# A routed expert layer with one static width for each place in an order by token count, and a second MLP whose first block runs in two parts

## The chip, the cores and the metric

The kernel runs on one core of one Trainium2 chip. The metric is the time of one execution on the device in microseconds (us). Lower is better.

## The reference

Three layers follow one another on 1536 tokens of 512 features. Only the second and the third are touched here.

```python
# 1. retention attention with a decay per head -> x [1536, 512]   (not touched)
# 2. each token goes to the one expert of 8 with the largest logit
logits = x @ w_gate                                # [1536, 8]
expert_idx = np.argmax(logits, axis=1)
gate_w = softmax(logits)[arange(N), expert_idx]
for e in range(8):
    mask = expert_idx == e
    h = np.maximum(x[mask] @ w1[e], 0.0)           # 512 -> 1024
    out[mask] = gate_w[mask, None] * (h @ w2[e])   # 1024 -> 512
# 3. a dense MLP
h = x @ w_in                                       # 512 -> 2048
return ((h - np.tanh(h)) @ w_out)                  # 2048 -> 512
```

`w_in` and `w_out` of the third layer arrive as float64, all other inputs as float32. With the inputs that the reference draws by default the eight experts get 195, 205, 194, 205, 168, 157, 227 and 185 tokens.

## The kernel before, in words

Every large product is taken in three matmuls: each float32 operand is split into a high part of TensorE's reduced float32 type (a cast on ACT) and a low part (the rest, a subtraction on DVE, both in `split`, L141 to L147), and high by high, low by high and high by low are added up in PSUM. So a weight tile costs one DMA, one ACT cast and one DVE subtraction before TensorE can use it. The weight tile is the stationary operand in the expert layer and in the first product of the second MLP; each matmul loads its own 128x128 weights.

The program has three stages.

The attention and routing stage handles 128 tokens in each of 12 steps. It finds each token's expert and its place there, and GpSimd scatters the scaled rows into `xs_d`, a DRAM buffer with room for 1536 rows of each expert (`scatter`, L62). It also decodes the first five of 32 float64 tiles.

The expert stage runs over n = 0 to 63: expert n // 8, feature tile n % 8 of 1024 = 8 x 128 (from L797). Each expert reads WT = 240 rows of its region of `xs_d` (`x_load`), transposes them on TensorE (`x_trans`), and multiplies with 240 moving columns for every expert. At step n, `e_first(n)` makes 12 matmuls with w1 and a ReLU, and `e_second(n - 2)` makes 12 with w2. The experts run in the order 0 to 7. After an expert's eighth tile its 240 result columns are copied from PSUM to `ysort` at the column `starts` of that expert (L639 on ACT, L641 on DVE); the next expert overwrites the columns beyond its count. `finish_routing` (L481) turns the eight counts into `starts` and a flag `over`, which is set if a count lies above WT or below 128; a second pass over windows of 256 tokens then replaces the result. The weights come by the queue of SyncE in the order of `fetch` (L787), some five steps ahead. The rows of an expert and the weights share that queue, and everything on it is issued in order.

The 32 float64 tiles are decoded beside this: `decode_load` (512 KB each, two buffers), `decode_math` (two ACT passes for the sign, two DVE passes for the bits), `decode_end` (an ACT pass for the magnitude and a GpSimd multiplication). One tile is decoded in every second step. From n = 52 on, once the last tile is decoded, `m_split` splits one tile in each step.

The second MLP (from L956) has three windows of 512 tokens and 16 feature tiles of 128 each: 48 steps. Step n is 12 matmuls `m_first` (L865), an approximation of h - tanh(h) in six ACT and six DVE operations (`g_head`, `g_body`, `g_high`, `g_low`), and, two steps later, 12 matmuls `m_second` (L945) that add up in four PSUM banks `outp` over the 16 tiles. The remaining splits of weight tiles are put into the DVE chain of a step as fillings: the list `fill` is taken from in two gaps of the chain of the next step, and what is left runs at its end. `pre` counts the tiles split so far; step n brings it to 2n + 8. `y_split` splits the tokens of the next window, and the last step of a window copies its four banks to `ysort` and scatters them to the output. All engine queues run in the order in which the program is written.

## Time and profile before

| | before |
|---|---|
| median of 3 runs | 561.08 us (560.43 to 564.28) |
| the profiled execution's own time | 558.93 us |
| span of its trace | 557.2 us |
| busy PE, PE weight loads, DVE, ACT, GpSimd | 95%, 83%, 82%, 67%, 21% |
| mean granted TensorE clock | 0.987 |

The profiled execution is 1.73 us longer than its span, and 2.15 us shorter than the median. PE is TensorE's matmul row, PEld its row of weight loads, which run beside the matmuls. Times in the rows below are microseconds from the start of the span unless marked ns; "L133" is line 133 of the kernel, and "x" counts instructions. A row's "idle before" is the time in which its engine waited, and the arrow names what it waited for.

### The profile page before, as it was taken

How to read it: one execution, taken by the hardware profiler on the slowest of the kernel's cores; microseconds unless marked ns; L12 is line 12 of the kernel's file. 1: busy time of each engine (PE TensorE's matmuls, PEld its weight loads, DVE VectorE, ACT ScalarE, POOL GpSimd, SP SyncE). 2: the span in 40 equal slices, each digit the busy share in tenths (PEclk: the TensorE clock that was granted, in tenths of full speed). 3: DMA queues.
4: the chain of work that ended last, by engine and by line, in shares of the span. 5: the costliest groups of instructions: out<-in, count | busy, mean ns of one | idle time of the engine just before them, and what ended most of it. 6: DMA issues, size and time to landing. Idle time of an engine off the chain costs nothing.

```text
span 557.2 us, 10218 instructions
## 1 busy us (share of the span) xinstructions
PE 530.3 (95%) x3709; PEld 465.1 (83%) x3709; DVE 455.3 (82%) x866; ACT 374.3 (67%) x750; POOL 114.5 (21%) x139
## 2 busy tenths in 40 slices
PE   6999889999999999999989999999999999999991
PEld 5878768999999999999968888888888888888881
DVE  5988896899989899899679988987767697767670
ACT  2445655698788799898577878765555676565650
POOL 3656444054434322321000000003000003000002
PEclk8899999999999999999999999999999999999997
DMA  5999574999999999993000000002000002000002
GB/s 136 266 280 271 150 226 151 339 323 288 319 287 266 292 315 333 289 340 116 1 0 1 1 2 0 1 0 78 0 2 0 1 1 76 0 1 0 1 1 81
DMA packets 75660, 72.89 MB, mean 131 GB/s; under 512 B 30160, under 2 KB 60880, under 8 KB 75600
## 3 DMA queue, kind: packets, MB, share of 16 engines
q1 hardware_dynamic: 73248, 65.84, 41.1%
q0 software_dynamic: 2352, 6.31, 3.1%
q8 instruction: 31, 0.51, 0.4%
q14 instruction: 29, 0.24, 0.2%
HBM read 63.73 MB, written 8.39 MB: 129 GB/s over the span
## 4 chain that ended last, share of the span: by engine, by line
PE 56%; issue 16%; DMA 11%; DVE 8%; ACT 5%; POOL 2%; SPq 1%; POOLq 0%; DVEq 0%; ACTq 0%
PE mhp L865 17%; PE outp L945 16%; PE yp L633 10%; PE ehp L606 3%; PE ehp L607 3%; PE ehp L605 3%; DMA w1r<-in_moe_w_dram 3%; DMA w2r<-in_moe_w_dram 3%; DVE at L288 2%; DMA tok_d<-toks,cpi 2%; ACT qt L247 2%; DMA k<-in_k_dram 1%; POOL out_dram L64 1%; DMA raw<-in_moe_w_in_dram 1%; DVE state L312 1%
## 5 line engine op out<-in xcount | busy, mean ns | idle before, releaser
L633 PE MATMUL yp<-hb,w2h 128*128 128x240 f32 x512 | 89.9, 276 | 0.0
L874 ACT ACTIVATE u<-mhp 128x512 f32<-128x512 f32 x48 | 28.7, 597 | 80.4 <-PE mhp L865 80.3
L865 PE MATMUL mhp<-yh,mh 128*128 128x512 f32 x192 | 75.2, 392 | 1.9 <-ACT yh L145 1.9
L633 PEld LDWEIGHTS yp<-hb,w2h 128*128 128x128 f32 x512 | 76.9, 189 | 0.0
L865 PE MATMUL mhp<-yh,ml 128*128 128x512 f32 x192 | 74.7, 389 | 0.0
L606 PE MATMUL ehp<-xh,w1l 128*128 128x240 f32 x256 | 71.2, 278 | 1.1 <-DVE w1l L146 0.7
L633 PE MATMUL yp<-hb,w2l 128*128 128x240 f32 x256 | 70.7, 276 | 1.4 <-DVE w2l L146 1.3
L605 PE MATMUL ehp<-xh,w1h 128*128 128x240 f32 x256 | 70.7, 276 | 0.0
L607 PE MATMUL ehp<-xl,w1h 128*128 128x240 f32 x256 | 70.3, 275 | 0.0
L896 DVE SCALAR_TENSOR_TENSOR s<-s,u 128x512 f32<-128x512 f32 x48 | 33.1, 690 | 45.3 <-ACT s L876 45.3
L64 POOL DMA_INDIRECT out_dram<-ysort,idx x12 | 11.7, 974 | 282.8 <-ACT ysort L950 279.1
L138 POOL TENSOR_TENSOR dw<-da,sg 128x512 f32<-128x512 f32 x32 | 43.9, 1372 | 104.1 <-ACT da L137 82.9
L945 PE MATMUL outp<-mh,gl 128*128 128x512 f32 x192 | 54.0, 395 | 0.0
L945 PE MATMUL outp<-ml,gh 128*128 128x512 f32 x192 | 54.0, 395 | 0.0
L945 PE MATMUL outp<-mh,gh 128*128 128x512 f32 x192 | 53.7, 394 | 0.0
L146 DVE TENSOR_TENSOR w1l<-w1r,w1h 128x512 fp32r<-128x512 f32 x64 | 51.4, 803 | 1.8 <-ACT w1h L145 0.4
L146 DVE TENSOR_TENSOR w2l<-w2r,w2h 128x512 fp32r<-128x512 f32 x64 | 52.4, 819 | 0.3
L865 PE MATMUL mhp<-yl,mh 128*128 128x512 f32 x192 | 51.7, 391 | 0.0
L606 PEld LDWEIGHTS ehp<-xh,w1l 128*128 128x128 f32 x256 | 48.2, 188 | 2.6 <-DVE w1l L146 2.5
L633 PEld LDWEIGHTS yp<-hb,w2l 128*128 128x128 f32 x256 | 48.2, 188 | 1.9 <-DVE w2l L146 1.9
L605 PEld LDWEIGHTS ehp<-xh,w1h 128*128 128x128 f32 x256 | 48.2, 188 | 0.0
L607 PEld LDWEIGHTS ehp<-xl,w1h 128*128 128x128 f32 x256 | 48.2, 188 | 0.0
(144 smaller groups left out, 1214.1 us busy)
## 6 DMA issues: line engine op xcount, KB each, us to landing
w1r<-in_moe_w_dram SPq DMA_DIRECT2D x64, 256.0 KB, 6.8
w2r<-in_moe_w_dram SPq DMA_DIRECT2D x64, 256.0 KB, 6.7
raw<-in_moe_w_in_dram SPq DMA_DIRECT2D x16, 512.0 KB, 7.3
raw<-in_moe_w_out_dram SPq DMA_DIRECT2D x16, 512.0 KB, 6.4
q<-in_q_dram SPq DMA_DIRECT2D x12, 256.0 KB, 5.2
v<-in_v_dram SPq DMA_DIRECT2D x12, 256.0 KB, 5.5
k<-in_k_dram SPq DMA_DIRECT2D x11, 256.0 KB, 5.1
xr<-xs_d SPq DMA_DIRECT2D x8, 256.0 KB, 7.2
```

The lines of the kernel that those rows point to most:

```text
L64: ins = pool.indirect_dma_start(out=dst[:, :], out_offset=bass.IndirectOffsetOnAxis(ap=ix.bitcast(U32), axis=0), in_=src, in_offset=None)
L138: pool.tensor_tensor(out=w, in0=a.bitcast(F32), in1=sg, op=ALU.mult)
L146: dve.tensor_tensor(out=lo, in0=src, in1=hi.bitcast(F32), op=ALU.subtract)
L247: act.copy(out=o, in_=src)
L605: pe.matmul(hp, lhsT=ah, rhs=xh, start=(kk == 0), stop=False)
L606: pe.matmul(hp, lhsT=al, rhs=xh, start=False, stop=False)
L607: pe.matmul(hp, lhsT=ah, rhs=xl, start=False, stop=(kk == KD - 1))
L633: pe.matmul(o, lhsT=a, rhs=b, start=(f == 0 and i == 0 and m == 0), stop=(f == EF - 1 and m == 2), skip_group_check=True)
L865: pe.matmul(hp[:, j, :], lhsT=a[:, sl], rhs=b, start=(i == 0), stop=(i == 3 * KD - 1))
L874: act.activation(out=u, in_=hp, func=ACTF.Square)
L896: dve.scalar_tensor_tensor(out=s1, in0=s1, scalar=B1, in1=u, op0=ALU.add, op1=ALU.mult)
L945: pe.matmul(outp[w][i], lhsT=a[:, sl], rhs=b, start=(fs[j] == 0 and m == 0), stop=done)
```

## The change

The experts get an order: expert 0 first, then the others by falling token count. `finish_routing` computes the rank of each expert by comparing a key (eight times the count, plus a tie break) pairwise, the start column of each by adding the counts of those in front, and sorts counts, expert numbers and starts by rank into `byrank`. The place in the order, not the expert, now has a static width: 240, 240, 220, 212, 206, 200, 196, 192. SyncE reads the expert number of a place from `byrank_i` into a register (`expert`) and addresses weights and rows with it. `finish_routing` moves from step 2 to the end of step 0, the rows of the second expert are loaded at step 1 instead of step 0, and at step 0 `fetch` stays within expert 0. Both halves of an expert's result are copied to `ysort` by ACT.

Of the 32 float64 tiles 24 are decoded in the expert stage. The eight others are loaded in the second MLP in halves of 256 KB, decoded at steps 2, 5, 8, 11, 13, 15, 17 and 19 with the bit operations as fillings (`late_work`), and split two steps later. The first window of the second MLP runs feature tiles 0 to 11, then the second window runs 0 to 15, then the first one 12 to 15, then the third. The first part's sums are parked in `ysort`, and DVE adds the second part's to them. Step n brings `pre` to n + 14, up to 24.

New allocations, the tables of the second pass and the same `ei`, `rows_of` and `WIDE` edits in further places are left out here.

```diff
--- before.py
+++ after.py
@@ -40,7 +40,11 @@
     EF = F // 128
     NF = FF // 128
     CAP = 256
-    WT = 240
+    NP = 12
+    ND = 2 * NP
+
+    WIDE = (240, 240, 220, 212, 206, 200, 196, 192)
+    WT = WIDE[0]
 
     const = ctx.enter_context(tc.tile_pool(name="const", bufs=1))
     small = ctx.enter_context(tc.tile_pool(name="small", bufs=2))
...
@@ -462,6 +471,13 @@
         pool.iota(ebase_i, pattern=[[NT, E]], base=0, channel_multiplier=0)
         dve.tensor_copy(out=ebase, in_=ebase_i)
         dve.tensor_copy(out=ebase_b, in_=ebase_i)
+        dve.tensor_scalar(out=riota, in0=ebase, scalar1=1.0 / NT, scalar2=0.25, op0=ALU.mult, op1=ALU.add)
+        dve.tensor_copy(out=byrank_i[:, 1, :], in_=riota)
+        dve.tensor_copy(out=riota, in_=byrank_i[:, 1, :])
+        dve.tensor_scalar(out=kadd, in0=riota, scalar1=-1.0, scalar2=float(E), op0=ALU.mult, op1=ALU.add)
+        dve.memset(kadd[:, 0:1], float(2 * E * NT))
+        for e in range(E):
+            pool.memset(wide_f[:, e:e + 1], float(WIDE[e]))
         pool.iota(slots_i, pattern=[[1, CAP]], base=1, channel_multiplier=0)
         dve.tensor_copy(out=slots, in_=slots_i)
         pool.iota(toks.rearrange("p (c b) -> p c b", b=B), pattern=[[C, NC], [S, B]], base=0, channel_multiplier=1)
@@ -482,16 +498,39 @@
         tp = bank([128, E], "tp")
         pe.matmul(tp, lhsT=ones_b, rhs=cnt, start=True, stop=True)
         dve.tensor_copy(out=ct, in_=tp)
-        inc = sm([128, E], F32, "inc")
-        dve.tensor_tensor_scan(out=inc, data0=ones[:, 0:E], data1=ct, initial=0.0, op0=ALU.mult, op1=ALU.add)
-        dve.tensor_tensor(out=starts, in0=inc, in1=ct, op=ALU.subtract)
-        dve.tensor_copy(out=starts_i, in_=starts)
-        cm = sm([128, 1], F32, "cm")
-        dve.tensor_reduce(out=cm, in_=ct, axis=AX.X, op=ALU.max)
-        dve.tensor_scalar(out=cm, in0=cm, scalar1=float(WT), scalar2=None, op0=ALU.is_gt)
+        page = slot([128, 512], F32, "page")
+        key = page[:, 0:E]
+        cmp = page[:, 64:128].rearrange("p (a b) -> p a b", b=E)
+        prod = page[:, 128:320].rearrange("p (v a b) -> p v a b", a=E, b=E)
+        rank = page[:, 320:320 + E]
+        sel_ = page[:, 384:448].rearrange("p (a b) -> p a b", b=E)
+        sq = [128, E, E]
+        dve.scalar_tensor_tensor(out=key, in0=ct, scalar=float(E), in1=kadd, op0=ALU.mult, op1=ALU.add)
+        dve.tensor_tensor(out=cmp, in0=key.unsqueeze(1).to_broadcast(sq), in1=key.unsqueeze(2).to_broadcast(sq), op=ALU.is_gt)
+        dve.tensor_reduce(out=rank, in_=cmp, axis=AX.X, op=ALU.add)
+        dve.tensor_tensor(out=cmp, in0=cmp, in1=ct.unsqueeze(1).to_broadcast(sq), op=ALU.mult)
+        dve.tensor_reduce(out=starts, in_=cmp, axis=AX.X, op=ALU.add)
+        dve.tensor_tensor(out=sel_, in0=rank.unsqueeze(1).to_broadcast(sq), in1=riota.unsqueeze(2).to_broadcast(sq), op=ALU.is_equal)
+        for i in range(3):
+            dve.tensor_tensor(out=prod[:, i], in0=sel_, in1=vals[:, i, :].unsqueeze(1).to_broadcast(sq), op=ALU.mult)
+        dve.tensor_reduce(out=byrank, in_=prod, axis=AX.X, op=ALU.add)
+        dve.tensor_copy(out=byrank_i, in_=byrank)
+        cm = sm([128, E], F32, "cm")
+        dve.tensor_tensor(out=cm, in0=byrank[:, 0, :], in1=wide_f, op=ALU.is_gt)
+        cx = sm([128, 1], F32, "cx")
+        dve.tensor_reduce(out=cx, in_=cm, axis=AX.X, op=ALU.max)
         few = sm([128, 1], F32, "few")
         dve.tensor_reduce(out=few, in_=ct, axis=AX.X, op=ALU.min)
-        dve.scalar_tensor_tensor(out=over, in0=few, scalar=128.0, in1=cm, op0=ALU.is_lt, op1=ALU.max)
+        dve.scalar_tensor_tensor(out=over, in0=few, scalar=128.0, in1=cx, op0=ALU.is_lt, op1=ALU.max)
+
+    eregs = {}
+
+    def expert(rank):
+        if rank == 0:
+            return slice(0, 1)
+        if rank not in eregs:
+            eregs[rank] = sp.value_load(byrank_i[0:1, 1, rank:rank + 1], min_val=0, max_val=E - 1)
+        return bass.ds(eregs[rank], 1)
 
     def token_table():
         dl = sm([128, E], F32, "dl")
@@ -516,14 +555,15 @@
         r = []
         for i in range(2):
             a = temp([128, DM], F32, "xr")
-            h = ROWS[i]
-            sp.dma_start(out=a[0:h, :], in_=xs_d[e * NT + i * 128:e * NT + i * 128 + h, :])
+            h = rows_of(e)[i]
+            sp.dma_start(out=a[0:h, :], in_=xs_d.rearrange("(e n) d -> e n d", n=NT)[expert(e), i * 128:i * 128 + h, :].rearrange("e n d -> (e n) d"))
             r.append(a)
         xrow[e] = r
 
-    ROWS = (128, WT - 128)
-
-    def x_trans(e, rows=ROWS):
+    def rows_of(e):
+        return (128, WIDE[e] - 128)
+
+    def x_trans(e, rows):
         r = xrow.pop(e)
         hs, ls = [], []
         for g in range(2):
...
@@ -634,11 +676,10 @@
                               skip_group_check=True)
         if f == EF - 1:
             yp = ys.pop(e)
-            at_ = starts_i[0:1, e:e + 1] if col is None else col
+            at_ = byrank_i[0:1, 2, e:e + 1] if col is None else col
             ra = act.value_load(at_, min_val=0, max_val=NT)
             act.copy(out=ysort[:, 0:2, bass.ds(ra, wd)], in_=yp[0][:, :, 0:wd])
-            rd = dve.value_load(at_, min_val=0, max_val=NT)
-            dve.tensor_copy(out=ysort[:, 2:4, bass.ds(rd, wd)], in_=yp[1][:, :, 0:wd])
+            act.copy(out=ysort[:, 2:4, bass.ds(ra, wd)], in_=yp[1][:, :, 0:wd])
 
 
     whl = {}
@@ -666,12 +707,12 @@
     nl = [0]
 
     def decode_fetch():
-        if nl[0] < min(nd[0] + 2, 2 * NF):
+        if nl[0] < min(nd[0] + 2, ND):
             decode_load(nl[0])
             nl[0] += 1
 
     def decode_step():
-        if nd[0] < 2 * NF:
+        if nd[0] < ND:
             decode_math(nd[0])
             nd[0] += 1
 
@@ -786,8 +827,9 @@
 
     def fetch(n):
         ahead = 5 if n < 36 else 4 if n < 44 else 3
-        while 2 * got[0] <= min(n + ahead + 3, NE - 2) or got[1] <= min(n + ahead, NE - 1):
-            if 2 * got[0] <= min(got[1] + 3, NE - 2):
+        end = EF if n == 0 else NE
+        while 2 * got[0] <= min(n + ahead + 3, end - 2) or got[1] <= min(n + ahead, end - 1):
+            if 2 * got[0] <= min(got[1] + 3, end - 2):
                 e_load1(got[0])
                 got[0] += 1
             else:
@@ -798,13 +840,11 @@
         LAG = 2
         for n in range(NE + LAG):
             if n < NE:
-                if n == 2:
-                    finish_routing()
                 if n == 4:
                     token_table()
                 if n >= 6 and n % 2 == 0 and n < 6 + 2 * (NTT + 1):
                     token_scatter((n - 6) // 2)
-                if n % EF == 0 and n // EF + 1 < E:
+                if n == 1 or n % EF == 0 and 0 < n // EF < E - 1:
                     x_load(n // EF + 1)
                 fetch(n)
                 if n == 0:
@@ -818,18 +858,20 @@
                     e_split1((n + 3) // 2, 0)
                 e_split2(n)
                 if n % EF == 4 and n // EF + 1 < E:
-                    x_trans(n // EF + 1)
+                    x_trans(n // EF + 1, rows_of(n // EF + 1))
                 decode_flush()
                 if n % 2 == 1:
                     decode_step()
                 else:
                     decode_fetch()
-                if n >= NE - 12 and nd[0] == 2 * NF:
+                if n >= NE - 12 and nd[0] == ND:
                     m_split(pre[0])
                     pre[0] += 1
+            if n == 0:
+                finish_routing()
             if n >= LAG:
                 e_second(n - LAG)
-        while nd[0] < 2 * NF:
+        while nd[0] < ND:
             decode_fetch()
             decode_step()
             decode_flush()
@@ -929,10 +971,11 @@
         o, width = wins[w]
         nt = width // 128
         gh, gl = ghl.pop((w, fs))
-        if fs[0] == 0:
+        if fs[0] in ((0, NP) if w == 0 else (0,)):
             outp[w] = [bank([128, DM], "outp") for _ in range(nt)]
         ops = [(i, j, m) for j in range(len(fs)) for m in range(3) for i in range(nt)]
-        last = fs[-1] == NF - 1
+        close = fs[-1]
+        last = close in ((NP - 1, NF - 1) if w == 0 else (NF - 1,))
         if w == len(wins) - 1 and fs[-1] >= NF - 3:
             ops.sort(key=lambda x: x[2] == 2)
         if last:
@@ -942,23 +985,23 @@
             a, b = ((gh, wh), (gh, wl), (gl, wh))[m]
             sl = slice(j * width + i * 128, j * width + (i + 1) * 128)
             done = last and j == len(fs) - 1 and m == 2
-            pe.matmul(outp[w][i], lhsT=a[:, sl], rhs=b, start=(fs[j] == 0 and m == 0), stop=done)
+            pe.matmul(outp[w][i], lhsT=a[:, sl], rhs=b, start=(fs[j] in ((0, NP) if w == 0 else (0,)) and m == 0), stop=done)
             if done:
-                kk, oc = i, (0, 512, 0)[w]
-                ob = ysort[:, kk, oc:oc + DM]
-                if i % 2 == 0 or nt == 2:
-                    act.copy(out=ob, in_=outp[w][i])
+                home = ysort[:, i, 0:DM] if w else ysort[:, i, DM:2 * DM]
+                if w == 0 and close == NF - 1:
+                    dve.tensor_tensor(out=home, in0=home, in1=outp[w][i], op=ALU.add)
+                elif i % 2 == 0:
+                    act.copy(out=home, in_=outp[w][i])
                 else:
-                    dve.tensor_copy(out=ob, in_=outp[w][i])
-                t = o // 128 + i
-                scatter("out" if fresh else "again", out, idx[:, t:t + 1], ob)
+                    dve.tensor_copy(out=home, in_=outp[w][i])
+                if close == NF - 1:
+                    t = o // 128 + i
+                    scatter("out" if fresh else "again", out, idx[:, t:t + 1], home)
 
     def second_mlp(fresh):
         seq = []
-        for w, (o, width) in enumerate(wins):
-            per = 512 // width
-            units = [tuple(range(f, f + per)) for f in range(0, NF, per)]
-            seq += [(w, fs) for fs in units]
+        for w, a, b in ((0, 0, NP), (1, 0, NF), (0, NP, NF), (2, 0, NF)):
+            seq += [(w, (f,)) for f in range(a, b)]
         LAG = 2
 
         def high(i):
@@ -973,6 +1016,54 @@
             lo = slot([128, 512], F32R, "ml")
             dve.tensor_tensor(out=lo, in0=w.rearrange("p k f -> p (k f)"), in1=hi.bitcast(F32), op=ALU.subtract)
             whl[i] = (hi, lo)
+
+        late = {}
+
+        def late_load(i):
+            f = i // 2
+            if i % 2 == 0:
+                src = w_in.bitcast(I32)[:, f * 256:(f + 1) * 256].rearrange("(k p) (f t) -> p k f t", p=128, t=2)
+            else:
+                src = w_out.bitcast(I32)[f * 128:(f + 1) * 128, :].rearrange("p (k f t) -> p k f t", k=KD, t=2)
+            late[i] = [slot([128, 2, 128, 2], I32, "late") for _ in range(2)]
+            for g in range(2):
+                sp.dma_start(out=late[i][g], in_=src[:, 2 * g:2 * g + 2])
+
+        def late_math(i, fill):
+            r = late.pop(i)
+            sg = slot([128, KD, 128], F32, "sg")
+            a = slot([128, KD, 128], I32, "da")
+            for g in range(2):
+                gs = slice(2 * g, 2 * g + 2)
+                lo, hi = r[g][:, :, :, 0], r[g][:, :, :, 1]
+                act.activation(out=sg[:, gs], in_=hi.bitcast(F32), func=ACTF.Identity, bias=SGN)
+
+                def bits(gs=gs, lo=lo, hi=hi):
+                    dve.tensor_scalar(out=a[:, gs], in0=hi, scalar1=3, scalar2=0x40000000, op0=ALU.logical_shift_left,
+                                      op1=ALU.bitwise_xor)
+                    dve.scalar_tensor_tensor(out=a[:, gs], in0=lo, scalar=29, in1=a[:, gs], op0=ALU.logical_shift_right,
+                                             op1=ALU.bitwise_or)
+
+                fill.append(bits)
+            act.activation(out=sg, in_=sg, func=ACTF.Sign, bias=-SGN)
+            late[i] = (sg, a)
+
+        def late_end(i):
+            sg, a = late.pop(i)
+            dec[i] = signed(a, sg)
+
+        def late_work(n, fill):
+            for j, at_ in enumerate((2, 5, 8, 11, 13, 15, 17, 19)):
+                i = ND + j
+                if n == max(at_ - 4, 0):
+                    late_load(i)
+                if n == at_:
+                    late_math(i, fill)
+                if n == at_ + 1:
+                    late_end(i)
+                if n == at_ + 2:
+                    high(i)
+                    fill.append(lambda i=i: low(i))
 
         y_split(0)
         while fresh and pre[0] < 2:
@@ -999,13 +1090,14 @@
             if kind == "F":
                 m_first(w, fs)
                 if n + 1 < len(seq) and seq[n + 1][0] != w:
-                    y_split(w + 1)
+                    y_split(seq[n + 1][0])
                 if n == len(seq) - 1:
                     continue
             g_head(w, fs)
             g_body(w, fs, fill, seq[n - 1] if n else None, n <= 4)
             if fresh:
-                while pre[0] < min(2 * n + 8, 2 * NF):
+                late_work(n, fill)
+                while pre[0] < min(n + 14, ND):
                     high(pre[0])
                     fill.append(lambda i=pre[0]: low(i))
                     pre[0] += 1
...
```

## Rows read from the trace of the kernel before

**Rows 1.** Busy time by stretch: length, then each engine with its instructions, clock, DMA.

```profile
94.10:278.20 184.10, 181.59 (x1596) 179.34 (x1594) 167.69 (x292) 150.59 (x307) 55.05 (x54) 1.00 0.88 267
200.00:220.00 20.00, 20.00 (x181) 20.00 (x180) 19.77 (x33) 18.96 (x39) 5.74 (x4) 1.00 0.97 310
278.80:546.00 267.20, 265.66 (x1152) 215.99 (x1152) 210.05 (x328) 177.22 (x326) 9.67 (x19) 1.00 0.02 9
420.00:440.00 20.00, 20.00 (x89) 16.29 (x88) 13.76 (x22) 11.49 (x22) 0.00 (x0) 1.00 0.00 0
```

**Rows 2.** Groups by shape, weight loads, whole span: busy us, mean ns | idle before.

```profile
L633 PEld LDWEIGHTS yp<-hb,w2l 128*128 128x128 f32 x256 | 48.2, 188 | 1.9 <-DVE w2l L146 1.9
L606 PEld LDWEIGHTS ehp<-xh,w1l 128*128 128x128 f32 x256 | 48.2, 188 | 2.6 <-DVE w1l L146 2.5
...
L364 PEld LDWEIGHTS lr<-wg,xt 128*128 128x128 f32 x8 | 1.0, 191 | 0.1
```

**Rows 3.** Timeline in the routing stage, PEld and PE: start, length, count.

```profile
87.35 0.97 PEld L364 LDWEIGHTS lr<-wg,xt 128*128 128x128 f32 x8
87.35 1.06 PE L364 MATMUL lr<-wg,xt 128*128 128x8 f32 x8
```

**Rows 4.** Waits of the queue of SyncE: us in total, times, longest.

```profile
SPq L520 <- DMA xs_d<-xg,posi: 7.2, 1, 7.2
```

**Rows 5.** The chain that ended last, its longest pieces: start, length, what.

```profile
101.66 6.65 DMA raw<-in_moe_w_in_dram
...
157.34 9.10 DMA w1r<-in_moe_w_dram
```

**Rows 6.** Timeline, DVE and ACT, 101 to 109 us.

```profile
101.73 0.16 DVE L484 COPY ct<-tp 128x8 f32<-128x8 f32 x1
...
102.85 0.16 DVE L494 SCALAR_TENSOR_TENSOR over<-few,cm 128x1 int32<-128x1 f32 x1
...
108.33 0.43 DVE L128 TENSOR_SCALAR da<-raw 128x512 int32<-128x512 int32 x1 [1.46 <-DMA raw<-in_moe_w_in_dram]
...
108.39 0.69 ACT L125 ACTIVATE sg<-raw 128x512 f32<-128x512 f32 x1 [4.00 <-DMA raw<-in_moe_w_in_dram]
```

**Rows 7.** Groups by shape on DVE, 94 to 278 us.

```profile
L146 DVE TENSOR_TENSOR w2l<-w2r,w2h 128x512 fp32r<-128x512 f32 x64 | 52.4, 819 | 0.3
...
L129 DVE SCALAR_TENSOR_TENSOR da<-raw,da 128x512 int32<-128x512 int32 x27 | 18.7, 692 | 0.9
L128 DVE TENSOR_SCALAR da<-raw 128x512 int32<-128x512 int32 x27 | 11.8, 436 | 4.0 <-DMA raw<-in_moe_w_in_dram 2.7 <-DMA raw<-in_moe_w_out_dram 1.2
...
L641 DVE COPY ysort<-yp 128x480 f32 x7 | 4.6, 657 | 1.1 <-PE ehp L607 0.4 <-issue 0.3
```

**Rows 8.** Timeline, DVE, ACT and PE, 280 to 282 us.

```profile
280.04 0.65 DVE L641 COPY ysort<-yp 128x480 f32 x1
...
280.73 1.14 ACT L145 CAST yh<-ysort 128x512 fp32r<-128x512 f32 x2 [1.40 <-DVE ysort L641]
...
281.40 0.50 PE L865 MATMUL mhp<-yh,mh 128*128 128x512 f32 x1 [1.29 <-ACT yh L145]
```

**Rows 9.** Timeline, GpSimd and DVE, 163 us.

```profile
163.22 1.30 POOL L138 TENSOR_TENSOR dw<-da,sg 128x512 f32<-128x512 f32 x1 [1.71 <-ACT da L137]
...
163.30 1.78 DVE L146 TENSOR_TENSOR w2l<-w2r,w2h 128x512 fp32r<-128x512 f32 x1
```

**Rows 10.** Timeline, DVE and PE, two steps of the second MLP.

```profile
323.53 0.69 DVE L896 SCALAR_TENSOR_TENSOR s<-s,u 128x512 f32<-128x512 f32 x1 [0.57 <-ACT s L876]
...
327.15 0.68 DVE L925 TENSOR_TENSOR gl<-s,gh 128x512 fp32r<-128x512 f32 x1
...
329.43 1.10 PE L945 MATMUL outp<-mh,gl 128*128 128x512 f32 x4
...
417.49 0.69 DVE L896 SCALAR_TENSOR_TENSOR s<-s,u 128x512 f32<-128x512 f32 x1 [1.40 <-ACT s L876]
...
420.29 0.68 DVE L925 TENSOR_TENSOR gl<-s,gh 128x512 fp32r<-128x512 f32 x1
...
423.38 1.10 PE L945 MATMUL outp<-mh,gl 128*128 128x512 f32 x4
```

43 lines of the change are left out of this document (26 added, 17 removed).

## The prediction

> **What bounds the kernel now.** I read busy time by stretch first, then the groups of weight loads, the chain, the waits, and the timeline where they point. The reader is to see two stages in which TensorE is nearly full, each at a limit of its own. In the expert stage a full stretch holds 180 weight loads and 181 matmuls in 20 us, so one pair every 0.111 us, and PEld is busy all the time; in the second MLP there are 88 to 89 in 20 us, one every 0.226 us [rows 1]. At 0.111 us the 1594 loads of the expert stage need 177.1 us of its 184.1: 7.0 us are lost. At 0.226 us the 1152 of the second MLP need 260.4 of 267.2, but its steady step is 5.53 us (worked out below), and 48 x 5.53 = 265.4, so about 2 us are lost there. The attention stage before 94 us is hardly touched.
>
> What sets the 0.111 us? In the routing stage four float32 matmuls move only 8 columns against 128x128 weights, recorded as eight pairs. Their eight loads take 0.97 us, and with 0.19 us for one that is (0.97 - 0.19) / 7 = 0.111 us from load to load [rows 2, 3]. One load lasts 191 ns there and 188 ns in the expert stage [rows 2]. So the weight load alone sets 0.111 us, whether 8 or 240 columns follow it. That is the row on which my forecast hangs.
>
> **The widths.** They go from 8 x 240 = 1920 to 1706 columns over the places, 214 fewer, each moved by 192 matmuls. With the load as limit this gives 0. The other bound is a limit by columns: from 240 to 512 columns the spacing grows by 0.115 us [rows 1], 0.00042 us a column, and 214 x 192 x 0.00042 = 17.3 us. I take 0, because the spacing at 8 columns equals that at 240. The Trainium skill (TensorE: Matmul & The Clock Gate, "Back-to-back issue gap") gives an isolated spacing of columns / 2.4 GHz + 2.5 ns, by which the change would save an estimated 17 us; the same page ("LDWEIGHTS (loading the stationary operand)") gives columns of weights / 1.2 GHz, 107 ns for 128, which would save nothing, and the eight-column row sides with the second.
>
> **The start of the expert stage.** Now SyncE holds the queue for 7.2 us at the second expert's rows until the routing's scatters have landed [rows 4], and everything behind waits: the seventh float64 tile is issued at 101.66 and needs 6.65 us [rows 5]; ACT idles 4.00 us and DVE 1.46 us for it [rows 6]. With `fetch` and that tile ahead of the rows, DVE gets its 1.46 us back: -1.5. Against that, `finish_routing` grows from 8 small DVE operations, 101.73 to 103.01 us or 0.16 each [rows 6], to 20, several on 64 to 192 elements. At 0.16 to 0.2 each the twelve more cost 1.9 to 2.4, I take 2.1. They now stand ahead of the w1 and w2 subtractions of step 1, which TensorE needs for `e_second(1)`; I count 1.8 us of waiting there. SyncE waits for `byrank_i`, and behind it rows and weights of place 1 and the float64 tile of step 2; the rows are needed at step 4. A transfer took 6.65 us in the crowded queue [rows 5]; the queue is nearly empty here, so I put that wait inside the 1.8. Sum +0.3, bounds -1.5 (the extra operations fall into room) and +4 (rows late too).
>
> **The rest of the expert stage.** Each place's end takes one copy of 0.657 us [rows 7] and its register load off DVE. What TensorE waits for in this stage is DVE's subtractions, 2.5 + 1.9 us [rows 2]. Seven times 0.657 = 4.6 us of DVE work against these 4.4 us of waits: I take a third, -1.5 (0 to -4.4). ACT takes the copy; it has 150.6 of 184.1 us in use [rows 1], so it hides. Decoding 24 tiles instead of 32 takes 8 x (0.692 + 0.436) = 9.0 us off DVE [rows 7], but from step 38 on; there TensorE is already at its loads, so 0. The transfers (4.2 MB less, 8 x 512 KB) go from the same late steps: the chain runs through weight transfers at 157 us [rows 5], and up to step 37 as much per step is asked of the queue as before. 0.
>
> **The entry to the second MLP.** The last copy on DVE sits behind two subtractions, at 280.04; ACT's cast waits 1.40 us for it and TensorE 1.29 us, until 281.40 [rows 8]. With ACT doing both copies in its own order this shrinks; one ACT pass of 0.57 (half of the 1.14) is added in front. I take -0.9 (-1.3 to 0).
>
> **Eight decodings in the second MLP.** A step is 5.53 us: the two chains shown begin 93.96 us apart, and 17 steps [rows 10]. The DVE chain leaves room in it. Without fillings the low part `gl` starts 2.80 us after the chain begins and ends 2.4 us before TensorE's first matmul with it; with two fillings 3.62 us after, and 1.6 us before [rows 10]. So two fillings cost 0.8 us of a cushion of 2.4. The bits of a tile cost 0.436 + 0.692 = 1.13 us [rows 7], about 1.25 in four halves. A GpSimd multiplication beside DVE stretches a subtraction to 1.78 us, 1.1 too long [rows 9]; on average the 64 subtractions of w2 take 819 ns [rows 7] against 0.68, 8.9 us lost in sum, and twice that if those of w1 lose as much: 17.8 / 27 = 0.65 us a tile. The Trainium skill (SBUF — State Buffer, "Who interferes with whom") calls this port an exclusive lock; taken as a whole multiplication of 1.30 us a tile, the extra work below would be 3.2 us more.
>
> Up to step 16, DVE gets 6 x 1.25 = 7.5 of bits, 5 x 0.65 = 3.2 of stretching, two parked sums of 0.68, and 17 instead of 21 low parts (-4 x 0.6): +9.7 us. Before, DVE waited 0.57 us for ACT at the start of a step with two fillings and 1.40 us without [rows 10]; with ten steps of one and four of the other, 11.3 us of room. It suffices in sum, unevenly in place. Walking the steps I find three late low or high parts: at step 1 (two fillings where there was none), 0.2; at step 4 (bits of step 2 still queued), 0.5; at step 10 (four subtractions of the next window, 4 x 0.6, on top of two fillings), 0.5. I take +1.2; bounds 0 (all in the room) and 9.7 - 2.4 = +7.3 (no room usable, only the cushion). The third change of window repeats what passes without loss twice now; ACT, with six of its passes and 5 more a tile, has 90 of 267 us free [rows 1]; the transfers meet an idle queue (2% busy, [rows 1]). 0 each. If DVE's room is gone, each of these costs what it takes.
>
> **Setup.** Five small DVE operations more in the attention stage, 0.1 to 0.2 each by the like of [rows 6]: +0.6 (0 to 1). The eight GpSimd fills are hidden there.
>
> **Sum:** 0 + 0.3 - 1.5 - 0.9 + 1.2 + 0.6 = -0.3 us. The profiled execution's 558.93 becomes 558.6; it stands 2.15 below the median, so 560.8 us against 561.08.
>
> **The rivals.** (1) Columns do set the spacing at 240, and 214 fewer count. For: 240 and 512 columns differ by 0.115 us, near what 272 columns take one by one at the granted clock of 1.00, which is 2.4 GHz (113 ns). Against: the eight-column row. Up to step 37 transfers hold, so 12 to 17 us: 544 to 549 us. Chance 0.05. The skill's isolated spacing above is this case. (2) The relief of DVE and the earlier transfers take away most of the 7.0 us lost in the expert stage, and nothing comes back: 553 to 555. For: all named waits there are DVE's. Against: up to step 37 transfers and decoding run as before. Chance 0.10. (3) Slower: DVE falls behind in steps 3 to 16 of the second MLP. It decides once DVE is more than 1.6 us late in a step with two fillings; each microsecond beyond is TensorE's. With 7.3 there and the gains elsewhere gone, 561.1 + 7.3 = 568. For: the decodings are densest where the splits still run. Against: 11.3 us of room. Chance 0.11. (4) SyncE's wait for the order makes the rows of place 1 and the next weights late: +4 to +7, 565 to 568. Chance 0.04; slower in half of it. (5) The widths don't hold and the second pass runs: expert stage and second MLP again, some 450 us more. The reference's counts in falling order behind expert 0 (195) are 227, 205, 205, 194, 185, 168, 157, all within their widths. Chance 0.01.
>
> **How the numbers follow.** A measurement of this kernel tells 1%, 5.6 us, from no change. My forecast, 560.8, has 0.69: its terms' bounds, not all at one end, give 556 to 566. Faster by over 1%: rivals 1 and 2, 0.15. Slower by over 1%: 3, half of 4, and 5, 0.14. Within: 0.71. The range reaches into rivals 2 and 3: 554 to 568.
>
> **What would show it.** Right: 180 weight loads in 20 us also at the places with 192 to 206 columns; the stage from the first expert matmul to the second MLP within 3 us of 184; no 4.00 us idle of ACT near 108; TensorE's gap before 281.40 shorter; late starts of matmuls with `gl` around steps 1, 4 and 10 only, under 2 us in sum. Wrong: spacing near 0.09 us at 192 columns (rival 1), `gl` as releaser of TensorE through steps 3 to 16 (rival 3), TensorE waiting for rows of place 1 (rival 4).

## The result, and the profile of the changed kernel

The change makes the kernel 1.4% slower: 570.11 us (median of 4, 569.5 to 570.97) against 561.88 (4 runs, 560.43 to 564.28), a ratio of 1.0143 with the 95% interval 1.0102 to 1.0185. The forecast was 560.8 with a range to 568.0. The profiled execution took 570.97 us, span 569.2. It lies at the upper end of its runs and the one of before (558.93) at the lower end of its own, so the two spans differ by 12.0 us where the medians differ by 8.2. What follows counts the second MLP from the trace, where the same code repeats to 0.1 us, and is careful with the expert stage, where the same code has taken 185.1 to 190.1 us.

Busy time by stretch for the changed kernel: the expert stage, two full stretches of it, the second MLP (columns as in [rows 1]).

```profile
94.40:284.50 190.10, 183.18 (x1595) 179.13 (x1594) 156.30 (x278) 138.40 (x292) 44.37 (x45) 1.00 0.80 241
200.00:220.00 20.00, 20.00 (x183) 20.00 (x182) 17.70 (x33) 16.22 (x36) 4.50 (x3) 1.00 1.01 327
260.00:280.00 20.00, 20.00 (x182) 20.00 (x181) 15.94 (x29) 13.36 (x29) 0.00 (x0) 1.00 0.26 80
284.50:557.30 272.80, 268.42 (x1150) 214.62 (x1151) 224.39 (x365) 192.44 (x362) 19.66 (x26) 1.00 0.06 18
```

Two things are to be seen. A full stretch still holds 181 to 182 weight loads, at 200 to 206 columns in the first of the two and in the narrowest places too (192 to 196 columns after 260 us), where 240 columns had 180 [rows 1]: the widths save nothing. And the second MLP, with the same 1152 matmuls, takes 272.8 us from its first weight load to its last, 6.5 more than before (266.3 by the same marks); DVE has 37 instructions more in it and ACT 36.

The waits of PEld show where those 6.5 us are. First the changed kernel from 284 to 558 us, then the kernel before from 278.8 to 546 (releaser, total, times, longest). They are counted at the weight load, which can run a little ahead, so they add up to more than TensorE loses.

```profile
PEld outp L988 <- DVE gl L967: 4.6, 9, 1.7
PEld outp L988 <- ACT gh L960: 4.0, 4, 1.1
PEld mhp L907 <- ACT yh L154: 1.9, 4, 0.7
PEld mhp L907 <- DVE ml L1017: 0.9, 1, 0.9
PEld outp L988 <- DVE ysort L992: 0.3, 1, 0.3
```

```profile
PEld mhp L865 <- ACT yh L145: 3.0, 4, 1.7
```

Before, nothing but the entry's and the windows' casts was waited for. Now the high part `gh` and the low part `gl` of a step's result h - tanh(h), which the second product of the MLP needs, are late thirteen times and one weight tile's low part once. By the distance from load to load beyond the usual 0.23 us the late starts are: 0.6 at step 1 (299 us), 0.2 and 0.4 at steps 4 and 5 (318 and 324), 0.9 and 1.6 at step 11 (342 and 358), on either side of the four subtractions for the next window (345 to 348), and then 0.2 to 0.4, 1.1, and 0.3 to 0.4 three times over (381 to 388, 394 to 401, 406 to 413): 3.7 in the first five and 5.2 in the last nine.

The last nine belong to one event that repeats. ACT, then DVE, then TensorE of the changed kernel around the first high part that is late, with ACT's first long wait ahead of it:

```profile
370.25 0.63 ACT L146 ACTIVATE da<-da 128x512 f32<-128x512 f32 x1 [3.66 <-DVE da L1044]
...
378.48 0.63 ACT L932 ACTIVATE m<-u 128x512 f32<-128x512 f32 x1
382.76 0.63 ACT L146 ACTIVATE da<-da 128x512 f32<-128x512 f32 x1 [3.65 <-DVE da L1044]
383.30 0.58 ACT L916 ACTIVATE u<-mhp 128x512 f32<-128x512 f32 x1
...
385.45 0.61 ACT L960 CAST gh<-s 128x512 fp32r<-128x512 f32 x1
```

```profile
377.71 0.68 DVE L1017 TENSOR_TENSOR ml<-sg,mh 128x512 fp32r<-128x512 f32 x1
378.31 0.68 DVE L942 SCALAR_TENSOR_TENSOR s<-s,s 128x512 f32<-128x512 f32 x1
378.92 0.28 DVE L1042 TENSOR_SCALAR da<-late 128x256 int32<-128x256 int32 x1
...
381.38 0.73 DVE L948 COPY_PREDICATED s<-m,mhp 128x512 f32<-128x512 int32 x1
381.99 0.28 DVE L1042 TENSOR_SCALAR da<-late 128x256 int32<-128x256 int32 x1
382.31 0.42 DVE L1044 SCALAR_TENSOR_TENSOR da<-late,da 128x256 int32<-128x256 int32 x1
```

```profile
378.75 1.08 PE L907 MATMUL mhp<-yl,mh 128*128 128x512 f32 x4
379.67 1.09 PE L988 MATMUL outp<-mh,gh 128*128 128x512 f32 x4
...
384.36 1.07 PE L907 MATMUL mhp<-yl,mh 128*128 128x512 f32 x4
386.11 1.20 PE L988 MATMUL outp<-mh,gh 128*128 128x512 f32 x4 [0.68 <-ACT gh L960]
```

In steps 13, 15, 17 and 19 the fill list, the DVE work that is slipped between the links of the activation chain, holds three entries: the low part of an earlier weight tile, then the two halves of the bits of a new one. The chain of the next step has two places for them, so the second half (382.31) runs only after that chain has ended. ACT's magnitude pass of that tile (line 146) needs both halves. It stands at the head of ACT's queue and waits 3.65 us for them; behind it stands `u` (line 916), the first pass of the next step, whose matmuls ended at 379.83. `u` starts at 383.30, `gh` follows 2.15 us later, and TensorE stands until 386.11. In the whole second MLP ACT waits 19.2 us for such bits, eight times; the four waits of 3.65 to 3.67 us are those of steps 13, 15, 17 and 19. Behind the first of the four (370.25) no high part is late; the other three hold up one each.

### The profile page after: what moved, and what is told of

Its sections match the earlier page's. It is cut to its first block, busy times and chain, and to the rows that moved or that the text cites. A ratio compares the mean times of both kernels' runs of the same rounds, so it can differ in the third digit from the quotient of the medians.

```text
span 569.2 us, 10548 instructions
## 1 busy us (share of the span) xinstructions
PE 536.2 (94%) x3709; PEld 464.6 (82%) x3709; DVE 458.9 (81%) x895; ACT 377.3 (66%) x770; POOL 114.7 (20%) x147
## 4 chain that ended last, share of the span: by engine, by line
issue 31%; PE 25%; DVE 9%; DMA 9%; ACT 9%; POOL 3%; SPq 1%; POOLq 0%; DVEq 0%; ACTq 0%
PE yp L675 8%; DMA w1r<-in_moe_w_dram 4%; PE mhp L907 4%; PE outp L988 4%; DMA raw<-in_moe_w_in_dram 3%; PE ehp L647 2%; PE ehp L648 2%; PE ehp L646 2%; POOL out_dram L68 2%; DMA w2r<-in_moe_w_dram 2%; DVE w2l L155 1%; ACT w1h L154 1%; ACT w2h L154 1%; ACT s L918 1%; ACT da L146 1%
## 5 line engine op out<-in xcount | busy, mean ns | idle before, releaser
L147 POOL TENSOR_TENSOR sg<-da,sg 128x512 f32<-128x512 f32 x32 | 43.1, 1348 | 262.6 <-ACT da L146 262.5
L675 PE MATMUL yp<-hb,w2h 128*128 128x240 f32 (+6 forms) x512 | 89.8, 275 | 0.0
L647 PE MATMUL ehp<-xh,w1l 128*128 128x240 f32 (+6 forms) x256 | 71.2, 278 | 2.8 <-DVE w1l L155 2.5
L675 PE MATMUL yp<-hb,w2l 128*128 128x240 f32 (+6 forms) x256 | 70.7, 276 | 2.5 <-DVE w2l L155 2.5
L646 PE MATMUL ehp<-xh,w1h 128*128 128x240 f32 (+6 forms) x256 | 70.7, 276 | 1.2 <-ACT w1h L154 1.2
L648 PE MATMUL ehp<-xl,w1h 128*128 128x240 f32 (+6 forms) x256 | 70.3, 275 | 0.0
L988 PE MATMUL outp<-mh,gl 128*128 128x512 f32 x192 | 55.4, 400 | 1.3 <-DVE gl L967 1.2
L155 DVE TENSOR_TENSOR w2l<-w2r,w2h 128x512 fp32r<-128x512 f32 x64 | 49.2, 768 | 0.5 <-ACT w2h L154 0.3
L988 PEld LDWEIGHTS outp<-mh,gl 128*128 128x128 f32 x192 | 35.4, 188 | 12.5 <-DVE gl L967 4.6
```

The source lines that it names most:

```text
L147: pool.tensor_tensor(out=sg, in0=a.bitcast(F32), in1=sg, op=ALU.mult)
L155: dve.tensor_tensor(out=lo, in0=src, in1=hi.bitcast(F32), op=ALU.subtract)
L646: pe.matmul(hp, lhsT=ah, rhs=xh, start=(kk == 0), stop=False)
L647: pe.matmul(hp, lhsT=al, rhs=xh, start=False, stop=False)
L648: pe.matmul(hp, lhsT=ah, rhs=xl, start=False, stop=(kk == KD - 1))
L675: pe.matmul(o, lhsT=a, rhs=b, start=(f == 0 and i == 0 and m == 0), stop=(f == EF - 1 and m == 2), skip_group_check=True)
```

## The experiments

Times are medians, with the ratio to the kernel before in runs on the same chip (its medians were 559.3 to 559.6). The first expectations count from the 561.9 us that the kernel before took in the result above, so a ratio times 561.9 is what they compare with. The stage lengths are from the traces, from the first weight load of the expert stage to the first of the second MLP, and from there to the last one with `outp`.

**Each part alone.** The order and the widths with the second MLP of before and all 32 tiles decoded in the expert stage:

```diff
-    NP = 12
-    ND = 2 * NP
+    ND = 2 * NF
...
-                late_work(n, fill)
-                while pre[0] < min(n + 14, ND):
+                while pre[0] < min(2 * n + 8, 2 * NF):
```

> Only the order of the experts and its widths; all 32 float64 tiles are decoded in the expert stage again, and the second MLP is that of before. In the trace after, the stretch from the first expert matmul to the second MLP is 5.4 us longer than before (190.1 against 184.7) and the second MLP 6.5 us longer. If the two parts cost by themselves, this kernel takes about 561.9 + 5.5 - 1 (the entry to the second MLP, where ACT now makes both copies) = 566 to 567, its expert stage 189 to 190. If the second part with its fewer decodings had been giving something back in the expert stage, it takes 569 or more; if the loss in the expert stage came from the second part, 561 to 562.

And the second part alone, on the old order:

```diff
+    NP = 12
+    ND = 2 * NP
...
+        for w, a, b in ((0, 0, NP), (1, 0, NF), (0, NP, NF), (2, 0, NF)):
+            seq += [(w, (f,)) for f in range(a, b)]
...
-                while pre[0] < min(2 * n + 8, 2 * NF):
+                late_work(n, fill)
+                while pre[0] < min(n + 14, ND):
```

> Only the second part: eight float64 tiles in the second MLP, first window split at 12; the experts and their widths as before. If the parts cost by themselves: expert stage 184 to 185 as before, second MLP 6 to 8 us longer than before's 266.3, in sum 568 to 570. If the second part is only bad because the expert stage hands over late, the second MLP is within 2 us of before and the sum 561 to 563.

The order alone: 559.57 us, ratio 0.9999 (0.9973 to 1.0025). The second part alone: 566.93, ratio 1.0135 (1.0092 to 1.0178). On the level of the expectations that is 561.9, the third of the outcomes named for the one, and 569.5, the first for the other. So nearly all of the loss came with the second part: 7.5 of 8.2 us. In the profile of the order alone the expert stage is 3.4 us longer than before (188.1), in a run that is itself 2.2 us above its median, and the second MLP, the code of before, takes 265.3 instead of 266.3: the shorter entry. The second part alone has 182.6 and 275.2 us; of the latter 1.4 are a fall of the clock (last section).

**The register.**

```diff
     def expert(rank):
-        if rank == 0:
-            return slice(0, 1)
-        if rank not in eregs:
-            eregs[rank] = sp.value_load(byrank_i[0:1, 1, rank:rank + 1], min_val=0, max_val=E - 1)
-        return bass.ds(eregs[rank], 1)
+        return slice(rank, rank + 1)
```

> The kernel after with the experts in the order 0 to 7, addressed without a register, all else kept, the 20 DVE operations too. It leaves out that rows and weights follow the computed order, so its output is that of wrongly placed experts. Theory 1 (the queue of SyncE stands from 93.6 to 103.4 us for the order, and the transfers, 1.5 MB behind at 104 us, hold the stage until step 37): the expert stage is 3 to 5 us shorter than after's 190.1, the time 565 to 567. Theory 2 (the twelve more DVE operations and their delay of the subtractions): the wait of 1.5 us at 102.6 stays and so does the rest, 569 to 570.5.

Measured 568.54, ratio 1.015 (1.0105 to 1.0195), which is 570.3 on the level of the expectation: theory 2, and within the interval of the changed kernel. The queue of SyncE in this kernel, around 100 us:

```profile
93.01 0.38 SPq L122 DMA_DIRECT2D raw<-in_moe_w_in_dram  x1
101.04 0.80 SPq L555 DMA_DIRECT2D xr<-xs_d  x2
```

With nothing to read from the order, SyncE still issues nothing from 93.0 to 101.0 us: it waits 7.6 us for the scatters of the token rows, as it waited 7.2 before [rows 4]. In the changed kernel it is released at 103.44. So the register adds about 2.4 us to a wait that is there anyway, and TensorE has not reached those rows. The same 1.2 us wait of TensorE stands in both kernels (at 104 us, below).

**The place of the bits.** In the changed kernel, the bits of a tile are put ahead of the low part of another in the same step:

```diff
                 if n == at_ + 1:
                     late_end(i)
+            for j, at_ in enumerate((2, 5, 8, 11, 13, 15, 17, 19)):
+                i = ND + j
                 if n == at_ + 2:
                     high(i)
                     fill.append(lambda i=i: low(i))
```

> The kernel after, but in a step of the second MLP that decodes one tile and splits another, the bit operations come ahead of the low part in the list of fillings. Theory 1 (at steps 16, 18 and 20 the second half of the bits stands at the end of the DVE chain, ACT's magnitude pass waits for it at the head of ACT's queue, and the next step's first ACT passes stand behind): the three waits of 1.06 us for the high part and some of those for the low part behind them go, 3 to 4.5 us, so 565.5 to 567. Theory 2 (DVE has simply too much to do, in whatever order): within 1 us of 570.1.

Beside the order of the fillings this puts one cast on ACT, the high part of the earlier tile, behind the sign passes of the new one. Measured 563.77, ratio 1.0087 (1.0062 to 1.0112): 4.4 us above the kernel before instead of 8.2, which is 566.8 on the level of the expectation, theory 1; the second MLP takes 268.6 instead of 272.8. The waits of PEld in its second MLP:

```profile
PEld outp L988 <- DVE gl L967: 2.3, 3, 1.7
PEld mhp L907 <- ACT yh L154: 1.9, 4, 0.7
PEld mhp L907 <- DVE ml L1017: 0.9, 1, 0.9
PEld outp L988 <- ACT gh L960: 0.7, 1, 0.7
PEld outp L988 <- DVE ysort L992: 0.3, 1, 0.3
```

All nine late starts between 381 and 413 us are gone, and nothing else, with not one instruction fewer. ACT waits 0.64 to 0.65 us for each of the four tiles instead of 3.65 to 3.67, and `u` waits for its matmuls again; the third of the four:

```profile
385.03 0.63 ACT L932 ACTIVATE m<-u 128x512 f32<-128x512 f32 x1
386.30 0.63 ACT L146 ACTIVATE da<-da 128x512 f32<-128x512 f32 x1 [0.65 <-DVE da L1044]
387.88 0.60 ACT L916 ACTIVATE u<-mhp 128x512 f32<-128x512 f32 x1 [0.94 <-PE mhp L907]
```

**The places of the decodings.** On top of that, the eight tiles are decoded in later steps, and the weight splits run ahead as they did before:

```diff
-            for j, at_ in enumerate((2, 5, 8, 11, 13, 15, 17, 19)):
+            for j, at_ in enumerate((9, 12, 14, 16, 18, 20, 22, 24)):
...
-                while pre[0] < min(n + 14, ND):
+                while pre[0] < min(2 * n + 8, ND):
```

> The kernel after with the bits first, the decodings at steps 9, 12, 14, 16, 18, 20, 22 and 24 instead of 2, 5, 8, 11, 13, 15, 17 and 19, and pre brought to 2n + 8 in step n, as before. In the run with the bits first the second MLP still lost 4.9 us in gaps between weight loads, 1.1 of them at the entry; the rest were a late high part at the second step (0.6), low parts at steps 4 and 5 (0.6), the low part of a weight tile needed at step 11 (0.9) and a low part beside the next window's subtractions (1.6). Theory 1 (all of these are the place of the work, not its amount): they go, and the second MLP takes 265 to 266 us, the whole 559 to 562 against about 560 before. Theory 2 (eight decodings are too much for DVE wherever they stand): 2 us or more of gaps remain, 562 to 565.

Measured 561.73, ratio 1.0036 (1.0012 to 1.006); the second MLP takes 266.1. Before the change it took 266.3, but with the longer entry; the order alone, with this kernel's entry and without decodings, has 265.3. So 0.8 us of the 7.5 are left. Busy time by stretch, and PEld's waits for low parts of the result that are left:

```profile
281.20:547.30 266.10, 265.70 (x1151) 215.61 (x1152) 228.14 (x365) 193.64 (x362) 19.74 (x26) 1.00 0.06 21
```

```profile
PEld outp L988 <- DVE gl L967: 1.0, 2, 0.5
```

DVE and ACT do the same 365 and 362 instructions in it as in the changed kernel, and no less busy time. So nearly all of the work has room; its order had not. Two edits were made at once here, and what each of them cured is not separated.

**Of the second part, the split alone:** all 32 tiles decoded in the expert stage, the first window in two pieces.

```diff
+    NP = 12
...
+        for w, a, b in ((0, 0, NP), (1, 0, NF), (0, NP, NF), (2, 0, NF)):
+            seq += [(w, (f,)) for f in range(a, b)]
```

> The kernel before with the first window of the second MLP split at tile 12, and nothing else: all 32 tiles are decoded in the expert stage, pre at 2n + 8. It has a third change of window, four more casts and subtractions of tokens, and four sums that are parked and added. If the third change repeats what the two others pass without loss: within 0.5 us of before in the second MLP (266.3), 559 to 561 in sum. If the parked sums and the added subtractions make low parts late: 1 to 3 us of gaps near steps 12 to 15 and 27 to 32.

Measured 560.00, ratio 1.0013 (0.9983 to 1.0044); the second MLP takes 267.4, 1.1 more: the size of the second expectation, but at steps 10 and 11. Its waits of PEld at the change of window (330 to 360 us):

```profile
PEld outp L948 <- DVE gl L927: 1.3, 2, 0.9
```

Before, there was no such wait: the weight splits run to step 12 and the first change of window came at step 16; at step 12 the two meet. That this meeting is the cause is not shown: with the later decodings the splits end at step 8, and two low parts are late at the same change all the same (0.5 and 0.4 us, the 1.0 above).

**The better half on the old order:** the kernel before with the mended second part, and the place's second copy on ACT.

```diff
-            rd = dve.value_load(at_, min_val=0, max_val=NT)
-            dve.tensor_copy(out=ysort[:, 2:4, bass.ds(rd, wd)], in_=yp[1][:, :, 0:wd])
+            act.copy(out=ysort[:, 2:4, bass.ds(ra, wd)], in_=yp[1][:, :, 0:wd])
...
```

> The kernel before (no order, 240 columns) with the second part in that mended form, and both copies of an expert's result on ACT. Theory 1: second MLP 265 to 266 us; expert stage 182 to 183 as in the run with the second part alone, 2 less than before, for the fewer decodings; the entry 1 less. In sum 1 to 3 us below before, 557 to 559. If fewer decodings give nothing, 559 to 560; if theory 2 holds, 561 to 563.

Measured 558.24, ratio 0.9972 (0.9947 to 0.9997), as theory 1 has it; the second MLP takes 266.3. But the expert stage takes 185.7 us, not 182 to 183, and of the 1.3 us gained about 0.9 are the entry (below). What the fewer decodings gave at this pace can't be told from nothing.

**What earlier relief of the expert stage is worth.** In that kernel, the nineteen tiles that are still decoded there are spread over steps 1 to 51 instead of 1 to 37:

```diff
-                if n % 2 == 1:
+                if n in [1 + k * 50 // 18 for k in range(19)]:
                     decode_step()
```

> The kernel before with the mended second part and both copies on ACT (0.9972 of before, 0.9947 to 0.9997), and in addition the 19 float64 tiles of the expert stage spread evenly over its steps 1 to 51 instead of one in every second step up to 37. If the time that the expert stage loses (7.7 us in gaps between weight loads in that run's trace, all of them before step 37) comes from the density of decoding beside the splits and transfers, the gaps shrink to 4 to 5 us, and the time to 555.5 to 557.5 where before takes 559.6. If they come from single meetings with GpSimd's work, wherever it stands, the gaps stay at 6 to 8 us, merely spread to step 51, and the time at 558 to 559.

Measured 556.15, ratio 0.994 (0.9915 to 0.9965): faster than both kernels. The expert stage takes 182.7 us, against 185.7 with the old pace, in one profile each. Waits of PEld in that stage, first with the pace of before, then spread:

```profile
PEld ehp L610 <- DVE w1l L150: 2.7, 9, 0.5
PEld yp L637 <- DVE w2l L150: 2.7, 5, 0.8
```

```profile
PEld ehp L610 <- DVE w1l L150: 1.9, 4, 0.6
PEld xtp L539 <- DMA xr<-xs_d: 1.1, 2, 0.6
```

The waits for the w2 subtractions are gone, and 1.1 us of waits for rows have come up. The tiles moved out are the room for this: with all 32 decoded by the end of the stage, one tile in every second step already runs to step 53.

**The same with the new order**, to price the order once more: the kernel with the later places of the decodings gets this edit too.

> The changed kernel with everything that helped so far: the bits of both tiles ahead of the high and low parts, the second MLP's decodings every second step, and the nineteen tiles of the expert stage spread over its steps 1 to 51. Beside the kernel that does the same in the old order of experts (556.15 us, ratio 0.994) only the order and the widths differ. Theory 'the order costs next to nothing': within 1.5 us of that kernel, 555 to 558, ratio 0.992 to 0.997. Rival 'the order costs some 3 us': the two mended kernels without the spreading stood at 561.73 with the order and 558.24 without it, and this pair would stand as they do: 559 to 560, ratio 0.999 to 1.001.

Measured 558.55, ratio 0.9978 (0.9961 to 0.9996): 2.4 us above the kernel in the old order, between the two expectations; the intervals just overlap. The pair without the spreading differs by 3.5 (561.73 and 558.24), and its intervals don't overlap. Within the new order the spreading is worth 3.2 us (561.73 to 558.55), clear of both intervals.

Both old-order kernels have the copy on ACT, which is part of the order's 0.9999 above; by load starts it is worth 0.9 us at the entry (from the last `yp` load to the thirteenth of the second MLP 5.35 us before, 4.42 with it). The traces show where the order costs. Its eight kernels reach step 8, the second place, 23.5 to 23.6 us after the first weight load of the stage, the five in the old order after 21.4 to 22.2. And they begin the stage later, but only a part of that is theirs: in five of the thirteen profiles the granted clock falls for a while between 90 and 95 us. That stretch in the changed kernel, and in the one with the bits first:

```profile
90.00:95.00 5.00, 4.98 (x31) 4.25 (x32) 3.00 (x13) 2.44 (x5) 2.08 (x3) 1.00 0.93 281
90.00:95.00 5.00, 4.71 (x20) 3.85 (x21) 2.17 (x14) 1.19 (x2) 2.08 (x3) 0.68 0.95 276
```

Where the clock stays at 1.00 there, four kernels with the order begin at 94.4 to 95.3 us, 94.8 in the mean, and four in the old order at 94.1 to 94.4, 94.2 in the mean. Where it falls to 0.66 to 0.68, four with the order begin at 96.3 to 96.4 and the one in the old order, the second part alone, at 95.8. So the order costs 0.6 us at the start, and the fall 1.6 in either order.

**The routing at step 2**, in the kernel without the register:

```diff
+                if n == 2:
+                    finish_routing()
...
-            if n == 0:
-                finish_routing()
```

> As the run without the register (experts 0 to 7, so wrongly placed rows), but the 16 DVE operations of the routing stand at step 2, where before had 8. In all runs with the order, with and without the register, TensorE waits 1.4 us at 102.6 to 104.6 for the low part of w2 of step 1, and step 8 begins 23.6 us after the first step, against 21.4 to 22.0 in the runs without the order. If it is the place of the routing (ahead of step 1's subtractions), that wait goes and step 8 begins at 21.5 to 22.5. If it is the number of operations, the wait moves and step 8 stays at 23 or more.

One run, 569.24. The wait moves with the operations and grows, and step 8 still begins 23.5 us after the first step. TensorE in the changed kernel, then in this one:

```profile
104.13 0.38 PE L675 MATMUL yp<-hb,w2l 128*128 128x240 f32 x1 [1.17 <-DVE w2l L155]
```

```profile
101.20 0.38 PE L643 MATMUL ehp<-xh,w1l 128*128 128x240 f32 x1 [0.35 <-DVE w1l L155]
109.13 0.38 PE L643 MATMUL ehp<-xh,w1l 128*128 128x240 f32 x1 [2.28 <-DVE w1l L155]
```

So it is the block of small operations in DVE's queue that is paid for, at either of its two places. That it costs more here has a reason of its own: one of the operations (L513) takes 1.26 us instead of 0.22, beside a multiplication of GpSimd.

**One place of 68 rows in its second half instead of 64:**

```diff
-    WIDE = (240, 240, 220, 212, 206, 200, 196, 192)
+    WIDE = (240, 240, 220, 212, 206, 200, 196, 196)
```

> The kernel after with 196 instead of 192 columns at the last place, so that its second row tile has 68 rows instead of 64. In after, the eight transposes of that place are 0.20 to 0.27 us apart, and those of the other places 0.1. If the 64 rows do it, they are 0.1 apart here, 1.0 us less at 246 to 250 us. If it is what runs beside them at step 52 (the first split of a float64 tile), they stay at 0.20 to 0.27. The time itself moves too little to be seen.

One run, 568.02; what it shows stands in the last section.

## Why the prediction was wrong, point by point

**The step that failed** is "ACT, with six of its passes and 5 more a tile, has 90 of 267 us free ... 0 each." ACT did have the time: with the bits first, the same passes cost TensorE nothing there. But one of the passes, the magnitude, needs work that DVE puts behind its chain in a step with three fillings, and what stands behind a waiting pass waits too: the matmuls that `u` needs had ended at 379.83, and it ran behind the magnitude, at 383.30. The Trainium skill states this order for ACT, DVE and GpSimd (Perfetto Trace Analysis, "Tensor Engine Instruction (MATMUL, LD_WEIGHTS)": strict FIFO), and the trace agrees. A sum of free time says nothing on that. This step was put at 0 and cost 5.2 us of late starts in the profile, shown by the kernel in which only the place of the bits (and one cast with it) differs: its second MLP is 4.2 us shorter, its excess over the kernel before 3.9. The whole term of the second MLP, +1.2 with bounds 0 and 7.3, came out at 7.5 (272.8 us against 265.3 in the order alone, which has the same entry): 4.2 by this step, 2.5 that went with the later places of the decodings, and 0.8 that stayed.

**Late high and low parts by DVE's own load.** The forecast was 0.2, 0.5 and 0.5 us at steps 1, 4 and 10. Measured: 0.6 at step 1, 0.6 at steps 4 and 5, and 0.9 + 1.6 at step 11, beside the next window's subtractions. The places were nearly right, the size was three times too small (3.7 for 1.2). Half of the 1.6 is a low part that was itself slow; GpSimd and DVE of the changed kernel there:

```profile
356.05 1.28 POOL L147 TENSOR_TENSOR sg<-da,sg 128x512 f32<-128x512 f32 x1 [16.73 <-ACT da L146]
356.42 1.45 DVE L967 TENSOR_TENSOR gl<-s,gh 128x512 fp32r<-128x512 f32 x1
```

Without GpSimd beside it this subtraction takes 0.68 us. The prediction had this stretching, at 0.65 us a tile, but spread it over the sum; it is 0.8 us at once, and three times it stands right ahead of a late start: here, at step 5 (322.32), and at 338.40, behind which DVE runs without a pause up to the weight tile's low part that is late at 342. A part of the loss is not the decodings at all: "the third change of window repeats what passes without loss twice now" was wrong. The split alone puts 0.4 and 0.8 us there. And the weight tile that was late at step 11 was split with less lead (`n + 14` against `2 * n + 8`), which the prediction did not weigh. What the lead and what the slow subtraction has in that 0.9 is not separated: the run that restores the lead moves the decodings too.

**Rival 3** had the sign and, by luck, about the time, 568. Its mechanism, DVE's room used up in sum, was not what happened: the same work in later steps costs 0.8 us (266.1 against 265.3). "It suffices in sum, unevenly in place" was the true half of the sentence, and too little was charged for it.

**The widths, 0:** right. 181 to 182 loads in 20 us at 192 to 206 columns, 180 at 240, and the order with its widths alone takes the time of before (0.9999); rival 1 falls. The spacing of 0.111 us is the weight load's at every width that occurs here. The Trainium skill (TensorE: Matmul & The Clock Gate, "LDWEIGHTS (loading the stationary operand)") has columns / 1.2 GHz, an estimated 107 ns for 128, and the trace agrees within 4%.

**The start, +0.3:** the cost was there, the gain was not. TensorE waits 1.17 us at 104.13 for the subtraction behind the routing, as forecast at 1.8; DVE in the changed kernel, the first and the last of the small operations and the subtraction behind them (8 operations ended at 103.01 before [rows 6]):

```profile
99.68 0.16 DVE L500 COPY vals<-tp 128x8 f32<-128x8 f32 x1
...
102.70 0.16 DVE L524 SCALAR_TENSOR_TENSOR over<-few,cx 128x1 int32<-128x1 f32 x1
102.78 0.69 DVE L155 TENSOR_TENSOR w1l<-w1r,w1h 128x512 fp32r<-128x512 f32 x1
103.39 0.68 DVE L155 TENSOR_TENSOR w2l<-w2r,w2h 128x512 fp32r<-128x512 f32 x1
```

They take 3.2 us instead of 1.3, 1.9 more for a forecast of 2.1. That is luck: the forecast counted 20 operations and 16 run, eight more than before, at 0.20 us each instead of 0.16. ACT's 4.00 us at 108 are gone, but step 8 still starts 1.6 us later than before. So the -1.5 did not arrive at TensorE; the term is about +1.6, within its bounds. Some 0.5 of it is not the routing: at 113.5 us a load waits 1.0 us for a subtraction instead of 0.5, behind a cast of 12 elements (L543) that took 1.26 us instead of 0.17 beside a multiplication of GpSimd.

**Setup, +0.6:** right, as far as the traces can tell. Over all profiles the means of the starts differ by 1.1 us (95.6 and 94.5); among those with the same granted clock at 90 to 95 us it is 0.6.

**The entry, -0.9:** right. TensorE's longest idle there fell from 1.29 us [rows 8] to 0.55, and the thirteenth load comes 4.27 us after the last of the expert stage instead of 5.35: -1.1.

**The rest of the expert stage, -1.5:** not shown. The changed kernel's profile has it longer (190.1 us), another with the same code there 185.1, before 184.7; the difference between profiles is as large as the term, and why that one profile is so long stays open. That the pace of the decodings sets waits there (rival 2's premise) is borne out by the spreading: 2.1 us in the old order (558.24 to 556.15, the intervals overlap) and 3.2 in the new one (they don't). But this change keeps their pace up to step 37, as the prediction said against rival 2, and so it didn't collect them.

**What stays open:** the order costs nothing measurable alone (0.15 us, interval -1.5 to 1.4), and 2.4 and 3.5 us in the two pairs in which both kernels copy on ACT. The traces name 1.6 us at the second place and 0.6 at the start, 2.2 together; less the 0.9 at the entry that is 1.3, inside the first interval. Whether the clock falls more often at 90 to 95 us with the order (four of eight profiles, one of five without) can't be told from so few.

## What to carry to other kernels

Before work goes into an engine's free time, look not only at how much there is but at what will stand at the head of the queue: an instruction that needs another engine's filler work holds up all behind it, and here two engines that were free for 18 and 29% of the stage held TensorE up for 4 us by the order of list entries. When fillers are appended to a list with limited places, put those that another engine waits for first. And look for the dense stretch: moving work to another stage paid little by itself here (0.9972, most of it the entry) and more when the rest was then spread over the steps that it left empty (0.994).
